# The first segment's layer norm: its root on ScalarE and VectorE, its loads on two queues, its order changed

## The chip, the cores and the metric

The kernel runs on one core of a Trainium2 chip. The metric is the device time of one execution in microseconds (us), lower is better. A core has five engines that work side by side, each with its own stream of instructions, taken in order: TensorE (PE, matrix multiplication; its weight loads are listed apart as PEld), VectorE (DVE), ScalarE (ACT), GpSimd (POOL) and SyncE (SP), which here only starts DMA transfers. ScalarE can start transfers too, from a queue of its own. Engines wait for each other and for transfers by semaphores.

## The reference

```python
x = A_x                                     # 2048 tokens of 640 features, bf16
xn = (x - mean(x)) / sqrt(var(x) + 1e-05)    # layer norm of each token
q, k, v = xn @ wq, xn @ wk, xn @ wv          # 32 heads of 20
# four segments of 512 tokens, in order:
#   p = softmax(q k^T / sqrt(20) + causal mask);  a_dot = p v
#   a_mem = phi(q) M / (phi(q) z + 1e-06)        # M, z: sums over earlier segments
#   o = g * a_mem + (1 - g) * a_dot              # g = sigmoid(beta)
#   M += phi(k)^T v ; z += sum of phi(k)
s = o @ wo
h = sigmoid(xn @ w_gate) * (xn @ w_up)       # 1536 wide
out = x + s * silu(h @ w_down)
```

## The kernel before

Tokens are handled in four segments of 512, each in four blocks of 128. The features (640) are five chunks of 128. A projection therefore is five matmuls that add into one PSUM tile. The PSUM tiles of all stages but the scores come from one ring of four buffers (`ps_d`).

The order of each engine's instructions is the order in which the program writes them (`manual_schedule`). The middle part of the program is written by a planner with due times (`TIMES`); the beginning, which the change touches, is written out by hand:

- Lines 137 to 164: the loads. All go out from SP's queue: x in blocks 0, 1, 2, then the first column half of `Wv`, x block 3, the second half of `Wv`, then `Wk`, `Wq` and `beta`. `load_x` (line 137) takes a list of blocks.
- Lines 166 to 183: GpSimd fills constants, among them `mhalf` (-0.5, the power of the root) and `ident` (for transposes).
- Lines 225 to 239: `ln_stats` (VectorE: two `bn_stats` over 320 columns each, then `bn_aggr`, which gives mean and variance `mv`), `ln_rstd` (GpSimd: add EPS, then power -0.5, giving `rs`), `ln_norm` (VectorE: subtract the mean, multiply by `rs`, giving `xn`).
- Line 246, `ln_transpose`: five transposes on TensorE into a PSUM tile `pT`, then a copy by ScalarE or VectorE into `xnT`. `first_transpose` (line 642) is the same for block 0, in two parts: three chunks copied by ScalarE, two by VectorE.
- Line 330, `do_V(n, j, half, engine)`: the V projection of a block for half of the columns (five matmuls of 320 columns into `psv`), copied by the engine named.
- Line 629, `keep_warm(k)`: k matmuls on a tile of zeros, whose results nobody reads.
- Lines 633 to 693: the order of the first segment. Statistics run one or two blocks ahead of the norm; then transposes and V projections alternate; then the five K projections (`do_K`, copied by VectorE) and the five Q projections (`do_Q`, copied by ScalarE) follow, both into `psq` tiles. Their weights are `Wk` and `Wq`. In between, ScalarE's queue starts the loads of `Wg` and `Wu` (1920 KB each), and GpSimd's `late_constants` (line 186) waits for the last `xn` before it fills the constants of later stages.
- Lines 694 to 709: `bound` (rows that bound the scores, by way of DRAM tile `Bd` into `QT`), gates, and the first five gate and up projections of the GLU (`gp`, `up`), with Tanh on ScalarE (`tg`, line 410) and a product on VectorE (`hT`, line 421).

Behind that the planner's part begins with the first scores (line 535). It mixes scores, attention, GLU and the next segments' projections; those segments' norms use `ln_stats`, `ln_rstd` and `ln_norm` as well, with GpSimd's power.

Of the kernel before, what the change touches and what calls it, by code (L numbers as in the profile page):

```python
# [9 lines left out]
P = 128  # L10
D = 640
# [9 lines left out]
EPS = 1e-5  # L21
SCALE = DH ** (-0.5)
HD = D // 2

BF = mybir.dt.bfloat16
F32 = mybir.dt.float32
ACT = mybir.ActivationFunctionType
# [28 lines left out]
def segment_units(n):  # L56
# [11 lines left out]
    stats0=(0.83, 1.2, 1.95, 3.9), stats=(-0.55, 0.42, 1.32, 3.57), norm=(5.2, 5.75, 6.03, 6.18),  # L68
# [13 lines left out]
def kernel(  # L82
# [14 lines left out]
    nc = tc.nc  # L97
# [3 lines left out]
    cpool = ctx.enter_context(tc.tile_pool(name="const", bufs=1))  # L101
    ps_s = ctx.enter_context(tc.tile_pool(name="ps_s", bufs=1, space=PSUM))
    ps_d = ctx.enter_context(tc.tile_pool(name="ps_d", bufs=4, space=PSUM))
    lnp = ctx.enter_context(tc.tile_pool(name="ln", bufs=2))
# [19 lines left out]
    xt_of, xnT_of = {}, {}  # L124

    def mm(out_, lhsT, rhs, start, stop):


        if not ORDER["columns"]:
            nc.tensor.matmul(out_, lhsT=lhsT, rhs=rhs, start=start, stop=stop, skip_group_check=True)  # L130
            return
        for r in range(4):
            cols = slice(32 * r, 32 * r + 32)
            nc.tensor.matmul(out_[cols], lhsT=lhsT[:, cols], rhs=rhs, start=start, stop=stop,  # L134
                             tile_position=(0, 32 * r), skip_group_check=True)

    def load_x(n, parts=((0, 4),)):
        if n not in xt_of:
            xt_of[n] = lnp.tile([P, 4, D], BF, name="xt4", bufs=3)
        src = x2[n * L:(n + 1) * L, :].rearrange("(j p) d -> p j d", p=P)  # L140
        for a, b in parts:
            nc.sync.dma_start(xt_of[n][:, a:b, :], src[:, a:b, :])

    def load_w(eng, dst, src):
        eng.dma_start(dst[:], src.rearrange("(c p) n -> p c n", p=P))
# [3 lines left out]
    Wv = cpool.tile([P, DC, D], BF, name="Wv")  # L149
# [5 lines left out]
    warm = stg.tile([P, 3 * L], BF, name="mn")  # L155
    nc.vector.memset(warm[:, 0:L], 0.0)
    beta_b = cpool.tile([P, H], BF, name="beta_b")
    for half, blocks in ((0, (0, 1, 2)), (1, (3,))):
        load_x(0, [(j, j + 1) for j in blocks])
        hs = slice(half * HD, (half + 1) * HD)  # L160
        nc.sync.dma_start(Wv[:, :, hs], A_wv[:, hs].rearrange("(c p) n -> p c n", p=P))
    load_w(nc.sync, Wk, A_wk)
    load_w(nc.sync, Wq, A_wq)
    nc.sync.dma_start(beta_b[:], A_beta.partition_broadcast(P))

    mhalf = cpool.tile([P, 4], F32, name="mhalf")
    nc.gpsimd.memset(mhalf[:], -0.5)
    ident = cpool.tile([P, P], BF, name="ident")
# [17 lines left out]
    def late_constants(after):  # L186
        nc.gpsimd.tensor_copy(Mbd[:, 0, 0:1], after[:, 0:1])
        nc.gpsimd.memset(Ind[:], -1.0)
        nc.gpsimd.affine_select(out=Ind[:], in_=Ind[:], compare_op=ALU.is_ge, fill=0.0, base=0,
                                pattern=[[P, DC], [-DH, 4], [-4 * DH, NG]], channel_multiplier=1)  # L190
        nc.gpsimd.affine_select(out=Ind[:], in_=Ind[:], compare_op=ALU.is_ge, fill=0.0, base=DH - 1,
                                pattern=[[-P, DC], [DH, 4], [4 * DH, NG]], channel_multiplier=-1)
        nc.gpsimd.memset(KT[:].bitcast(mybir.dt.uint32), 0x3F803F80)
        ones_columns(1)
        nc.gpsimd.memset(obs[0][:], 0.0)
        nc.gpsimd.memset(Mbd[:], 1.0)
        for c, (h0, h1) in enumerate(HEADS):
            t = Mbd[:, c, :].rearrange("p (h e) -> p h e", e=E1)
            base = P * c - DH * h0
            nc.gpsimd.affine_select(out=t, in_=t, compare_op=ALU.is_ge, fill=0.0, base=base,  # L200
                                    pattern=[[-DH, 8], [0, E1]], channel_multiplier=1)
            nc.gpsimd.affine_select(out=t, in_=t, compare_op=ALU.is_ge, fill=0.0, base=DH - 1 - base,
                                    pattern=[[DH, 8], [0, E1]], channel_multiplier=-1)
        for r, c0, c1, w in WINDOWS:
            rows = slice(32 * r, 32 * r + 32)
            nc.gpsimd.tensor_copy(BD[rows, c0:c1, :], Mbd[rows, c0:c1, w * E1:w * E1 + WIN])
        nc.gpsimd.memset(Mbd[:], 0.0)
# [17 lines left out]
    def ln_stats(n, j, mv):  # L225
        st = lnp.tile([P, 2, 6], F32, name="st")
        for i in range(2):
            nc.vector.bn_stats(st[:, i, :], xt_of[n][:, j, i * HD:(i + 1) * HD])
        nc.vector.bn_aggr(mv[:, j, :], st[:])

    def ln_rstd(mv, rs, sl):
        nc.gpsimd.tensor_scalar(rs[:, sl], mv[:, sl, 1], EPS, None, op0=ALU.add)
        nc.gpsimd.tensor_tensor(rs[:, sl], rs[:, sl], mhalf[:, sl], op=ALU.pow)

    def ln_norm(n, j, mv, rs):
        xn = lnp.tile([P, D], BF, name="xn", bufs=2)
        nc.vector.tensor_scalar(xn[:], xt_of[n][:, j, :], mv[:, j, 0:1], rs[:, j:j + 1],
                                op0=ALU.subtract, op1=ALU.mult)
        return xn

    def ln_tiles(n):
        mv = lnp.tile([P, 4, 2], F32, name="mv")
        rs = lnp.tile([P, 4], F32, name="rs")
        return mv, rs

    def ln_transpose(n, j, xn, eng):
        if n not in xnT_of:
            xnT_of[n] = xpool.tile([P, DC, L], BF, name="xnT")
        pT = ps_d.tile([P, DC, P], BF, name="pT", tag="d")
        for c in range(DC):  # L250
            nc.tensor.transpose(pT[:, c, :], xn[:, c * P:(c + 1) * P], ident[:])
        dst = xnT_of[n][:, :, j * P:(j + 1) * P]
        if eng is nc.scalar:
            nc.scalar.copy(dst, pT[:])  # L254
        else:
            nc.vector.tensor_copy(dst, pT[:])
# [10 lines left out]
    def new_seg(n):  # L267
        seg[n] = dict(kt=stg.tile([P, DC, L], BF, name="ktd"),
                      kabs=stg.tile([P, DC], F32, name="kabs", bufs=2), hT=[], aa={}, odot=None)
# [60 lines left out]
    def do_V(n, j, half, evac):  # L330
        ps = ps_d.tile([P, HD], F32, name="psv", tag="d")
        for k in range(DC):
            mm(ps[:], xnT_of[n][:, k, j * P:(j + 1) * P], Wv[:, k, half * HD:(half + 1) * HD],
               k == 0, k == DC - 1)
        dst = V[n % 2][:, j, half * 16:(half + 1) * 16, 0:DH]
        src = ps[:].rearrange("p (h e) -> p h e", e=DH)
        if evac is nc.scalar:
            nc.scalar.copy(dst, src)
        else:
            nc.vector.tensor_copy(dst, src)  # L340
# [288 lines left out]
    def keep_warm(k):  # L629
        for _ in range(k):  # L630
            nc.tensor.matmul(wps[:], lhsT=warm[:, 0:P], rhs=warm[:, 0:L], start=True, stop=True)

    keep_warm(11)
    mv, rs = ln_tiles(0)
    new_seg(0)
    xns = {}

    def stats0(j):
        ln_stats(0, j, mv)
        ln_rstd(mv, rs, slice(j, j + 1))  # L640

    def first_transpose():

        xnT_of[0] = xpool.tile([P, DC, L], BF, name="xnT")
        for c0, c1 in ((0, 3), (3, 5)):
            pT = ps_d.tile([P, c1 - c0, P], BF, name="pT", tag="d")
            for c in range(c0, c1):
                nc.tensor.transpose(pT[:, c - c0, :], xns[0][:, c * P:(c + 1) * P], ident[:])
            dst = xnT_of[0][:, c0:c1, 0:P]
            if c0:  # L650
                nc.vector.tensor_copy(dst, pT[:])
            else:
                nc.scalar.copy(dst, pT[:])

    def norm0(j):
        xns[j] = ln_norm(0, j, mv, rs)

    stats0(0)
    stats0(1)
    norm0(0)  # L660
    first_transpose()
    load_w(nc.scalar, Wg, B_w_gate)
    stats0(2)
    norm0(1)
    keep_warm(2)
    do_V(0, 0, 0, nc.scalar)
    ln_transpose(0, 1, xns[1], nc.scalar)
    load_w(nc.scalar, Wu, B_w_up)
    stats0(3)
    norm0(2)  # L670
    do_V(0, 0, 1, nc.scalar)
    do_V(0, 1, 0, nc.scalar)
    ln_transpose(0, 2, xns[2], nc.scalar)
    norm0(3)
    late_constants(xns[3])
    do_V(0, 1, 1, nc.scalar)
    do_V(0, 2, 0, nc.scalar)
    ln_transpose(0, 3, xns[3], nc.scalar)
    do_V(0, 2, 1, nc.scalar)
    do_V(0, 3, 0, nc.scalar)  # L680
    do_V(0, 3, 1, nc.scalar)
# [7 lines left out]
    relayout(0, 0, Kd, KT, nc.sync)  # L689
    relayout(0, 0, Qd, QT, nc.sync)  # L690
    load_x(1)
    for c in range(3, 5):
        do_Q(0, c, nc.scalar)
# [46 lines left out]
    for p in range(0, OLD, 5):  # L740
        n, g = units[p][0], units[p][1][0][0]
# [22 lines left out]
    st = {}  # L764
# [12 lines left out]
    for n in range(NSEG):  # L777
# [52 lines left out]
        if n + 2 < NSEG:  # L830
            on("load_x", 0, load_x, (n + 2,))
# [106 lines left out]
```

## Time and profile before

| | |
|---|---|
| median of 3 runs | 322.85 us (322.77 to 323.37) |
| the profiled execution | 323.07 us |
| its span, from first to last instruction | 321.3 us |
| TensorE clock granted, mean | 1.00 |
| HBM read and written | 19.90 MB and 14.78 MB |
| ScalarE's idle time before its first copy of `xnT` | 4.2 us |
| VectorE's wait for the first x block | 2.0 us |
| VectorE's idle time before the first copy of K | 5.3 us |

How to read what the prediction shows: in the table of busy times, each engine has busy time, share of the span and count of instructions. In the chain of waits, each line is the start (us from the start of the span), the duration, and what the end of the kernel hung on in that stretch: an engine with tile and source line, or a transfer. It is followed back from the last instruction. In the timeline each line has start, duration, engine, source line, operation, output <- inputs, shapes and count, and in brackets the idle time of the engine just before and what ended it; the engine ACTq or SPq is the issue of a transfer. In the list of groups, the figures behind the bar are busy time in us and mean ns of one, then idle time before them. "issue" is time in which the engine waited for nothing that the profile shows.

### The profile page before, as it was taken

The page shows a single profiled execution, that of the slowest core. Times are in us where ns is not written, and L with a number is a line of the kernel's source. Part 1 is how long each engine was busy: PE and PEld are TensorE (multiplying, and loading weights), DVE is VectorE, ACT ScalarE, POOL GpSimd, SP SyncE. Part 2 cuts the span into 40 slices and gives each one's busy share as a digit, 9 for nine tenths or more (in the row PEclk, how much of TensorE's full clock was granted, in tenths as well). Part 3 has the DMA queues.
Part 4 walks back from the last instruction along what each step waited for, and adds up shares of the span by engine and source line. Part 5 has one row for each costly group of instructions (what it writes and reads, how often), then busy time and mean ns, then how long its engine had stood idle before and what let it go on. Part 6 is the DMA issues. An engine that isn't in the chain of part 4 may idle for free.

```text
span 321.3 us, 10065 instructions
## 1 busy us (share of the span) xinstructions
PE 313.3 (98%) x4247; PEld 167.2 (52%) x4247; DVE 229.8 (72%) x501; ACT 223.6 (70%) x221; POOL 137.6 (43%) x232
## 2 busy tenths in 40 slices
PE   7999999999999999999998999999999999999995
PEld 2544434665545445654565455545466655445673
DVE  5284265765779888997778999977787686744465
ACT  2623468788798777777897868779797775777630
POOL 4870035525273445335453364444633353535322
PEclk9999999999999999999999999999999999999999
DMA  7987479330742462506593482435554000270312
GB/s 216 380 333 182 133 158 339 119 57 2 210 153 61 91 173 84 124 22 194 160 212 96 114 121 94 114 109 174 138 140 128 23 22 22 103 146 4 98 19 82
DMA packets 55797, 41.36 MB, mean 129 GB/s; under 512 B 26920, under 2 KB 54376, under 8 KB 55752
## 3 DMA queue, kind: packets, MB, share of 16 engines
q1 hardware_dynamic: 54440, 36.78, 43.1%
q10 hardware_dynamic: 1312, 3.93, 3.1%
q8 instruction: 33, 0.54, 0.7%
q14 instruction: 12, 0.10, 0.1%
HBM read 19.90 MB, written 14.78 MB: 108 GB/s over the span
## 4 chain that ended last, share of the span: by engine, by line
PE 92%; DVE 2%; ACT 2%; POOL 1%; issue 1%; DMA 1%; DVEq 0%; ACTq 0%
PE yp L130 11%; PE up L130 11%; PE gp L130 10%; PE psq L130 9%; PE Sps L535 8%; PE gp L134 6%; PE up L134 5%; PE yp L134 5%; PE ApsT L559 5%; PE psv L130 4%; PE psq L134 4%; PE sp L130 3%; PE sp L134 3%; PE psv L134 1%; PE sp L516 1%; ACT pt L543 1%
## 5 line engine op out<-in xcount | busy, mean ns | idle before, releaser
L543 ACT ACTIVATE pt<-Sps 128x2048 bf16<-128x2048 f32 (+1 forms) x81 | 150.3, 1856 | 42.5 <-PE Sps L535 38.9
L545 POOL TENSOR_SCALAR_AFFINE_SELECT pt<-pt 128x512 bf16<-128x512 bf16 x128 | 82.7, 661 | 160.1 <-ACT pt L543 160.0
L421 DVE SCALAR_TENSOR_TENSOR hT<-tg,up 128x512 bf16<-128x512 bf16 x48 | 32.3, 673 | 23.1 <-PE up L130 8.5
L130 PE MATMUL up<-xnT,Wu 128*128 128x512 bf16 x160 | 43.0, 380 | 0.1
L130 PE MATMUL yp<-Wd,hT 128*128 128x320 bf16 x257 | 40.3, 300 | 1.2 <-issue 1.2
L410 ACT ACTIVATE tg<-gp 128x512 bf16<-128x512 f32 x48 | 28.6, 596 | 16.7 <-PE gp L130 12.7
L130 PE MATMUL gp<-xnT,Wg 128*128 128x512 bf16 x150 | 39.3, 380 | 0.0
L535 PE MATMUL Sps<-QT,KT 23*128 23x128 bf16 (+3 forms) x512 | 32.7, 301 | 0.1
L578 DVE STREAM_TRANSPOSE obT<-ob 128x512 bf16<-128x512 bf16 x30 | 21.1, 704 | 12.8 <-POOL ob L574 12.8
L130 PEld LDWEIGHTS <-hT 128*128 128x128 bf16 x257 | 23.5, 98 | 13.1 <-issue 4.5
L438 DVE SCALAR_TENSOR_TENSOR aa<-t,yp 128x320 bf16<-128x320 bf16 x32 | 15.4, 481 | 13.9 <-ACT t L437 13.7
L134 PE MATMUL gp<-xnT,Wg 128*32 128x512 bf16 x360 | 24.1, 380 | 0.0
L580 DVE STREAM_TRANSPOSE tb<-ApsT 128x512 f32<-128x512 f32 x30 | 21.2, 708 | 3.2 <-PE ApsT L559 3.0
L130 PEld LDWEIGHTS <-Wu 128*128 128x128 bf16 x160 | 14.4, 97 | 16.3 <-issue 3.2
L559 PE MATMUL ApsT<-pt,V 128*32 128x512 bf16 (+2 forms) x480 | 22.8, 299 | 0.0
L130 PEld LDWEIGHTS <-Wg 128*128 128x128 bf16 x150 | 14.0, 98 | 16.3 <-issue 2.2
L535 PEld LDWEIGHTS <-KT 23*128 23x128 bf16 x512 | 9.7, 92 | 24.4 <-issue 24.1
L134 PE MATMUL up<-xnT,Wu 128*32 128x512 bf16 x320 | 21.7, 380 | 0.0
L437 ACT ACTIVATE t<-yp 128x320 bf16<-128x320 f32 x32 | 13.9, 435 | 10.8 <-PE yp L130 9.0
L130 PE MATMUL psv<-Wv,xnT 128*128 128x320 bf16 x130 | 20.9, 299 | 0.4 <-ACT xnT L254 0.3
L574 POOL TENSOR_TENSOR ob<-tb,rb 128x320 bf16<-128x320 f32 x27 | 19.7, 731 | 2.2
L134 PE MATMUL yp<-Wd,hT 128*32 128x320 bf16 x508 | 20.2, 300 | 0.0
(114 smaller groups left out, 448.4 us busy)
## 6 DMA issues: line engine op xcount, KB each, us to landing
KT<-Kd SPq DMA_DIRECT2D x32, 80.0 KB
QT<-Qd SPq DMA_DIRECT2D x32, 80.0 KB
out_dram<-xt SPq DMA_DIRECT2D x15, 160.0 KB
Wg<-in_B_w_gate_dram ACTq DMA_DIRECT2D x1, 1920.0 KB
Wu<-in_B_w_up_dram ACTq DMA_DIRECT2D x1, 1920.0 KB
xt<-in_A_x_dram SPq DMA_DIRECT2D x3, 640.0 KB
Wd<-in_B_w_down_dram SPq DMA_DIRECT2D x1, 1920.0 KB
Xd<-xn SPq DMA_DIRECT2D x12, 160.0 KB
```

What stands on the lines that cost most here:

```text
L130: nc.tensor.matmul(out_, lhsT=lhsT, rhs=rhs, start=start, stop=stop, skip_group_check=True)
L134: nc.tensor.matmul(out_[cols], lhsT=lhsT[:, cols], rhs=rhs, start=start, stop=stop, tile_position=(0, 32 * r), skip_group_check=True)
L410: nc.scalar.activation(tg[:], gp[:], ACT.Tanh, scale=0.5)
L421: nc.vector.scalar_tensor_tensor(out=h[:], in0=seg[n]["tg"][:], scalar=1.0, in1=up[:], op0=ALU.add, op1=ALU.mult)
L438: nc.vector.scalar_tensor_tensor(out=s["aa"][j][:, hs], in0=t2[:], scalar=1.0, in1=yp[:], op0=ALU.add, op1=ALU.mult)
L535: nc.tensor.matmul(Sps[:, r, c0:c0 + ncol], lhsT=KT[32 * r:32 * r + DH + 3, g, kb * P:(kb + 1) * P], rhs=QT[32 * r:32 * r + DH + 3, g, q0: ...
L543: nc.scalar.activation(pt[:, :, 0:ntot], Sps[:, :, 0:ntot], ACT.Exp, scale=SCALE)
L545: nc.gpsimd.affine_select(out=pt[:, :, c0:c0 + P], in_=pt[:, :, c0:c0 + P], compare_op=ALU.is_ge, fill=0.0, base=0, pattern=[[0, 4], [1, P ...
L559: nc.tensor.matmul(ps[32 * r:32 * r + 32, q0:L], lhsT=Vflat[n % 2][:, off:off + 32], rhs=t[:, r, c0:c0 + ncol], start=(i == 0), stop=(i == ...
L574: nc.gpsimd.tensor_tensor(ob[:, :, 0:DH], tb[:, :, 0:DH], rb[:].unsqueeze(2).to_broadcast([P, L // 32, DH]), op=ALU.mult)
L578: nc.vector.transpose(s["obT", g // 4][:, g % 4, :], ob[:].rearrange("p b e -> p (b e)"))
L580: s["turn", g] = (lambda: nc.vector.transpose(tb[:].rearrange("p b e -> p (b e)"), ps[:]), quotients, turn_back)
```

## The change

Only the first segment is touched. Its loads are divided among SP's and ScalarE's queues, and block 0 is loaded in two column halves, one from each queue. Its root is no longer GpSimd's add and power: ScalarE takes a square root with EPS as bias (`root0`, from a tile `epsc` that GpSimd fills), and VectorE takes the reciprocal at the head of `norm0`. Statistics are written out by halves and stand elsewhere in VectorE's order. The transposes of block 3 move ahead of `do_V(0, 2, 0)`, and their copy goes to VectorE. Nine instead of eleven warm matmuls stand at the beginning. The later segments keep GpSimd's root.

```diff
-    def load_x(n, parts=((0, 4),)):
+    def load_x(n, a=0, b=4, cols=slice(0, D), eng=nc.sync):
...
-        for a, b in parts:
-            nc.sync.dma_start(xt_of[n][:, a:b, :], src[:, a:b, :])
+        eng.dma_start(xt_of[n][:, a:b, cols], src[:, a:b, cols])
...
-    for half, blocks in ((0, (0, 1, 2)), (1, (3,))):
-        load_x(0, [(j, j + 1) for j in blocks])
+
+    def load_wv(half, eng):
         hs = slice(half * HD, (half + 1) * HD)
-        nc.sync.dma_start(Wv[:, :, hs], A_wv[:, hs].rearrange("(c p) n -> p c n", p=P))
+        eng.dma_start(Wv[:, :, hs], A_wv[:, hs].rearrange("(c p) n -> p c n", p=P))
+
+    load_x(0, 0, 1, slice(0, HD))
+    load_x(0, 0, 1, slice(HD, D), nc.scalar)
+    load_x(0, 1, 2)
+    load_wv(0, nc.scalar)
+    load_x(0, 2, 3)
+    load_x(0, 3, 4, eng=nc.scalar)
+    load_wv(1, nc.sync)
...
+    epsc = cpool.tile([P, 1], F32, name="epsc")
+    nc.gpsimd.memset(epsc[:], EPS)
...
-    keep_warm(11)
+    keep_warm(9)
     mv, rs = ln_tiles(0)
     new_seg(0)
-    xns = {}
-
-    def stats0(j):
-        ln_stats(0, j, mv)
-        ln_rstd(mv, rs, slice(j, j + 1))
+    xns, sts = {}, {}
+
+    def half_stats0(j, i):
+        if i == 0:
+            sts[j] = lnp.tile([P, 2, 6], F32, name="st")
+        nc.vector.bn_stats(sts[j][:, i, :], xt_of[0][:, j, i * HD:(i + 1) * HD])
+        if i == 1:
+            nc.vector.bn_aggr(mv[:, j, :], sts[j][:])
+
+    def root0(j):
+        nc.scalar.activation(rs[:, j:j + 1], mv[:, j, 1:2], ACT.Sqrt, bias=epsc[:])
...
     def norm0(j):
+        nc.vector.reciprocal(rs[:, j:j + 1], rs[:, j:j + 1])
         xns[j] = ln_norm(0, j, mv, rs)
 
-    stats0(0)
-    stats0(1)
+    half_stats0(0, 0)
+    half_stats0(0, 1)
+    root0(0)
+    half_stats0(1, 0)
     norm0(0)
+    half_stats0(1, 1)
     first_transpose()
+    root0(1)
+    norm0(1)
     load_w(nc.scalar, Wg, B_w_gate)
-    stats0(2)
-    norm0(1)
+    half_stats0(2, 0)
+    half_stats0(2, 1)
     keep_warm(2)
     do_V(0, 0, 0, nc.scalar)
     ln_transpose(0, 1, xns[1], nc.scalar)
+    root0(2)
     load_w(nc.scalar, Wu, B_w_up)
-    stats0(3)
     norm0(2)
+    half_stats0(3, 0)
+    half_stats0(3, 1)
     do_V(0, 0, 1, nc.scalar)
     do_V(0, 1, 0, nc.scalar)
     ln_transpose(0, 2, xns[2], nc.scalar)
+    root0(3)
     norm0(3)
     late_constants(xns[3])
     do_V(0, 1, 1, nc.scalar)
+    ln_transpose(0, 3, xns[3], nc.vector)
     do_V(0, 2, 0, nc.scalar)
-    ln_transpose(0, 3, xns[3], nc.scalar)
     do_V(0, 2, 1, nc.scalar)
     do_V(0, 3, 0, nc.scalar)
     do_V(0, 3, 1, nc.scalar)
```

## The prediction

> **What bounds the kernel now.** I read the page's busy times first, then the chain of waits in order of time, then the timeline of the first 30 us, then the groups for single prices.
>
> ```profile
> span 321.3 us, 10065 instructions
> PE 313.3 (98%) x4247; PEld 167.2 (52%) x4247; DVE 229.8 (72%) x501; ACT 223.6 (70%) x221; POOL 137.6 (43%) x232
> ```
>
> TensorE is busy for all but 8.0 us of the span. Whatever delays its dense stream delays the end; other engines matter only where TensorE waits for them. The chain of waits says where that is:
>
> ```profile
> 0.80 2.40 DMA xt<-in_A_x_dram
> ...
> 3.21 0.90 DVE st L228 x2
> ...
> 4.13 0.22 DVE mv L229
> ...
> 4.44 0.26 POOL rs L232
> ...
> 4.77 0.59 POOL rs L233
> ...
> 5.39 0.46 DVE xn L237
> ...
> 13.25 1.53 PE psv L130 x10
> 14.78 10.79 PE psq L130 x50
> ```
>
> Up to about 10 us the chain hops from the first load over VectorE and GpSimd to the first transposes and back; from 14.78 us it is TensorE almost alone until 316 us. Among TensorE's waits the profile blames only one behind 14.78 us on another engine (cps, 0.3 us); the other, 1.2 us, is issue. So the measure of this change is one moment: when the K projections (psq) begin, 14.62 us by the timeline. All behind it should shift rigidly. The timeline's anchors are:
>
> ```profile
> 0.79 1.28 ACT L653 ACT_TABLE_LOAD   x1 [0.79 <-PEq L922]
> 5.89 0.45 PE L648 MATMUL pT<-ident,xn 128*128 128x128 bf16 x5 [0.40 <-DVE xn L237]
> 8.08 0.45 PE L251 MATMUL pT<-ident,xn 128*128 128x128 bf16 x5 [0.34 <-DVE xn L237]
> 8.57 0.69 ACT L254 COPY xnT<-pT 128x640 bf16<-128x640 bf16 x1 [0.37 <-PE pT L251]
> 10.01 0.44 PE L251 MATMUL pT<-ident,xn 128*128 128x128 bf16 x5
> 11.97 0.44 PE L251 MATMUL pT<-ident,xn 128*128 128x128 bf16 x5
> 14.62 5.56 PE L130 MATMUL psq<-xnT,Wk 128*128 128x512 bf16 x25
> 26.69 0.60 ACT L410 ACTIVATE tg<-gp 128x512 bf16<-128x512 f32 x1 [0.49 <-PE gp L130]
> ```
>
> Call the four groups of transposes T0 to T3: 5.89, 8.08, 10.01, 11.97. The table load at 0.79 waits for nothing: ScalarE is idle until 6.27.
>
> **The change, part by part.**
>
> *Root.* The path loses GpSimd's add and power: from mv0 at 4.34 to the norm at 5.39 is 1.05 us. It gains a Sqrt on ScalarE and a reciprocal on VectorE. No Sqrt stands in the trace. Nearest is a 128x32 Tanh; the reciprocal has rows at 16 and 8 elements:
>
> ```profile
> L216 ACT ACTIVATE th<-beta_b 128x32 f32<-128x32 bf16 x1 | 0.2, 221 | 0.0
> L567 DVE RECIPROCAL rb<-tb 128x16 f32<-128x16 f32 x30 | 7.4, 248 | 0.4
> L618 DVE RECIPROCAL rd<-Aps 128x8 f32<-128x8 f32 x2 | 0.4, 200 | 0.0
> ```
>
> Sqrt: 0.22, the ScalarE row with the fewest columns; bounds 0.15 (VectorE's copy of 8 columns, 147 ns) and 0.37 (ScalarE's copy of 256 columns). Reciprocal: 48 ns less for 8 elements fewer gives 0.16 for one; bounds 0.10 and 0.20. A crossing between engines is 0.03 to 0.10 here (mv to GpSimd 0.10, GpSimd to norm 0.04, xn to PE 0.05); I take 0.08 into ScalarE and 0.05 out. Without anything else block 0 would gain 1.05 - (0.08 + 0.22 + 0.05 + 0.16 + 0.02) = 0.52 us.
>
> *Table load.* Sqrt makes a second function set necessary. In the built program ScalarE's order is three DMA issues, the wait for mv0, the table load, Sqrt: the Sqrt has two waits (mv0 and GpSimd's epsc), the first stands alone ahead of the load. So the load no longer hides in the idle start; its 1.28 us fall behind mv0. Block 0: mv0 4.34, ScalarE awake 4.42, load to 5.70, Sqrt 5.72 to 5.94, reciprocal 5.99 to 6.15, norm 6.17 to 6.62 (0.45), T0 6.67 instead of 5.89: +0.78.
>
> The Trainium skill (ScalarE: Activation LUTs, What ACT_TABLE_LOAD costs) says a switch costs a load of about 1.28 us and a drain of 1.38 us, 2.66 us together, and its next section advises against mixing exp and sqrt. The trace has the same 1.28 and shows no drain, as nothing ran before; by the page's sum the forecast below would be 1.4 us higher.
>
> *Second load.* The first Tanh needs the old set again; its load stands behind the last Q copy. There ScalarE idles 0.49 us before tg at 26.69, so tg comes 0.8 us late and hT (27.85, waiting for up) some 0.3 us late; with th in between, cb 0.4 late. TensorE doesn't wait for these: its next buffers are due a microsecond later. Bd<-cb waits in the queue behind the 640 KB x load in any case (issued 29.16, its readers at 34.35). Cost 0; without that cover 0.4, since the first scores start right behind the bound rows.
>
> *Blocks 1 to 3.* VectorE now stops at each reciprocal until ScalarE has done the root, and ScalarE does it only behind the copy of the block before. Behind the waiting reciprocal stand the norm, the next statistics and the copy of xnT. Block 1: second statistics 6.62 to 7.07, mv1 7.30; ScalarE copies xnT 7.05 to 7.53 (T0 + 0.38, 0.48 long), root 7.55 to 7.77, reciprocal to 7.98, norm 8.00 to 8.39 (0.39), T1 8.44 (+0.36: some of the delay goes into the 0.34 us for which PE waited there). Block 2: copy of xnT1 8.93 to 9.62 (T1 + 0.49, 0.69), root 9.64 to 9.86, reciprocal to 10.07, norm to 10.49 (0.40), T2 10.54 (+0.53); before, this norm was done at 9.37, long ahead. Block 3: copy of xnT2 11.06 to 11.76, root to 12.00, reciprocal to 12.21, norm to 12.66 (0.39 to 0.45), T3 12.72.
>
> *T3 ahead of V(2,0).* Before, V(1,1) and V(2,0) stood between T2 and T3. Now only V(1,1) does, done at 10.54 + 0.39 + 0.69 = 11.62; so TensorE idles about 1.1 us for T3. Behind it come four half V's of 0.69 (14.62 - 13.25 = 1.37 for two) after T3's 0.39: psq at 12.72 + 0.39 + 2.74 = 15.85, against 14.62: **+1.23 us**. Block 3's copy moves to VectorE (some 0.7 us), hidden behind V(2,0) and V(2,1); ScalarE is spared one copy where it had time.
>
> *Loads.* SP loses three issues of about 0.45, ScalarE gains three, done by 2.2, when it is idle. First bytes move at 1.8 to 2.0 and x0's 164 KB are in by 2.5; its statistics began at 3.21. Two halves at once share the same DMA engines: gain between -0.2 (smaller packets) and +0.3 us; I take 0. Now Wv0 (410 KB) runs beside x1 and x2. At the 224 GB/s of the slowest stretch at nearly full DMA share (3.0 to 3.2 us), x1 with an equal share of Wv0 is in by 1.85 + 492/224 + 0.65 = 4.7, wanted at 6.0; both halves of Wv with all of x (1474 KB) by 9.1, wanted at 8.83: 0 to 0.3 lost; 0 taken, as the mean rate of the first 7 us was higher. Wg and Wu are issued 1.4 to 2 us later, behind roots, but last bytes were in by about 22.5 and gp begins at 25.4. GpSimd's late constants start 2 us later and have until 24.7 (KT's memset, done at 13.8 before) or much longer.
>
> *Two warm matmuls fewer.* The last warm ones end near 5.0; T0 at 6.67 leaves TensorE idle 1.7 us, against 0.40 before. The page grants full clock in every slice, yet the weight loads of the warm matmuls come 0.43 us apart, and 11 took only 4.25 us, so the last ran at half that: full speed came near 4.85, 3.5 us after the start. Nine just reach it. I take 0; a clock lost again costs up to half of another 3.5 us, 1.75.
>
> The Trainium skill (TensorE: Matmul & The Clock Gate, What's actually happening) puts the fall back after an idle window of about 3.4 us, which 1.7 us wouldn't fill; but it says that the window runs free, so a shorter burst may miss it.
>
> **Sum.** The profiled execution took 323.07: span 321.3 and 1.77 around it. Span 321.3 + 1.23 = 322.53, with 1.77 is 324.30. That execution lay 0.22 above the median of the runs, 322.85, so I forecast 322.85 + 1.23 = **324.1 us**. Each root and each reciprocal counts four times, since T0 to T3 hang on each other: Sqrt of 0.15 gives -0.3, of 0.37 +0.6; reciprocals -0.24 to +0.16; landing -0.3 to +0.2; Wv up to +0.3. They will not all fall to one side: about +0.6 to +2.1, 323.4 to 324.9.
>
> **Rivals.** (1) *The load is off the path* (not slower). If the table is in by 4.4, because ScalarE's load somehow runs ahead of the wait, the same sum gives T0 5.4, T1 7.2, T2 9.3; the T3 chain is 0.5 to 0.7 longer than before, and psq starts at 14.6: 322.9, or 322.5 if the halves also land 0.3 sooner. For it: ScalarE idles from 2.2 on. Against: the order in the program. It decides from a load that ends by 4.42. (2) *TensorE turns cold* in the 1.7 us gap or doesn't get warm: V groups of 1.3 instead of 0.69 in the first 3 us, part of it hidden in the waits for T1 to T3; about +1.0: 325.1, at most 325.9. For it: nine matmuls end just after the change of pace. Against: the gaps of 0.40 and 0.34 us before did no harm, and only one is longer now. That the change doesn't do what it says is excluded by the program's order.
>
> **Numbers.** Forecast 0.70, rival (1) 0.16, rival (2) 0.14. A measurement of this kernel can tell 0.2% (0.65 us) from no change. The forecast's low end is within it (0.05 of 0.70); rival (1) is mostly no change (0.12), some faster (0.04). Slower 0.65 + 0.14 = 0.79, same 0.17, faster 0.04. The range, 323.2 to 325.2, leaves out most of (1) and the worst of (2).
>
> **What would show it.** ACT_TABLE_LOAD starting at about 4.4, a second one before the first tg; T0 to T3 near 6.7, 8.4, 10.5, 12.7; TensorE idle for about 1.1 us ahead of T3, released by xn; psq at 15.9; its spacing behind unchanged. It is wrong if the load starts near 2, if psq starts before 15.2, or if the span grows by something else than psq's delay.

## The result, and the profile after

The changed kernel takes 324.06 us (median of 12 executions, 323.01 to 325.72); the kernel before, run beside it, 323.11 (12 executions, 322.77 to 324.22). The ratio is 1.0032, 95% interval 1.0016 to 1.0048: slower by 0.5 to 1.6 us. The profiled execution of the changed kernel is the slowest of its twelve, 325.72, with a span of 324.0 us; that has to be kept in mind in what follows.

The busy times of the changed kernel's page:

```profile
span 324.0 us, 10039 instructions
PE 312.1 (96%) x4216; PEld 168.0 (52%) x4245; DVE 230.9 (71%) x506; ACT 225.1 (69%) x225; POOL 134.6 (42%) x225
```

TensorE does the same work less two warm matmuls, and idles 11.9 us instead of 8.0 by the trace. Part of the difference probably only seems so: 29 more matmul records are missing here, 13 of them of `up`, and the trace has six idle stretches of 0.16 us ahead of `up` that the trace of before doesn't have. The chain of waits of the changed kernel (start, duration, what) shows where the front spends its time:

```profile
3.14 0.90 DVE st L651 x2
...
4.07 0.22 DVE mv L653
...
4.36 1.28 ACT L656
5.65 0.30 ACT rs L656
...
5.98 0.17 DVE rs L672
...
6.18 0.46 DVE xn L247
...
6.68 0.71 PE pT L664 x5
```

The line `ACT L656` of 1.28 us, right behind `mv` and ahead of the root `rs`, is the table load. GpSimd is gone from the chain (it had 0.26 and 0.59 there), and a load of 1.28, a root of 0.30 and a reciprocal of 0.17 have come instead. The timeline of the changed kernel gives the anchors, first ScalarE's load and Sqrt, then TensorE:

```profile
4.36 1.28 ACT L656 ACT_TABLE_LOAD   x1 [4.36 <-DVE mv L653]
5.65 0.29 ACT L656 ACTIVATE rs<-mv,epsc 128x1 f32<-128x1 f32 x1
...
1.24 4.02 PE L641 MATMUL wps<-mn 128*128 128x512 bf16 x9 [1.24 <-DVE mn L155]
6.68 0.71 PE L664 MATMUL pT<-ident,xn 128*128 128x128 bf16 x5 [1.42 <-DVE xn L247]
7.19 1.06 PE L641 MATMUL wps<-mn 128*128 128x512 bf16 x2
8.04 1.54 PE L130 MATMUL psv<-Wv,xnT 128*128 128x320 bf16 x5
...
11.77 0.45 PE L261 MATMUL pT<-ident,xn 128*128 128x128 bf16 x5
12.06 0.84 PE L130 MATMUL psv<-Wv,xnT 128*128 128x320 bf16 x5
13.96 0.45 PE L261 MATMUL pT<-ident,xn 128*128 128x128 bf16 x5 [1.06 <-DVE xn L247]
...
16.97 5.56 PE L130 MATMUL psq<-xnT,Wk 128*128 128x512 bf16 x24
```

T0 stands at 6.68, as worked out. But its five transposes take 0.71 us where before they took 0.45, two warm matmuls 1.06 instead of 0.59, five matmuls of V 1.54 instead of 0.84: TensorE runs at half pace here, until about 10 us. So this execution shows both the wait for the table and the second rival, and its K projections begin at 16.97 instead of 14.62. The wait ahead of T3 (13.96) is there too, 1.06 us, released by `xn`.

### The profile page after: what moved, and what is told of

It reads as the page before. It is cut to its first block, busy times and chain, and to the rows that moved or that the text cites. A ratio compares the mean times of both kernels' runs of the same rounds, so it can differ in the third digit from the quotient of the medians.

```text
span 324.0 us, 10039 instructions
## 1 busy us (share of the span) xinstructions
PE 312.1 (96%) x4216; PEld 168.0 (52%) x4245; DVE 230.9 (71%) x506; ACT 225.1 (69%) x225; POOL 134.6 (42%) x225
## 4 chain that ended last, share of the span: by engine, by line
PE 78%; DMA 7%; ACT 5%; DVE 5%; issue 2%; SPq 2%; POOL 1%; ACTq 0%; DVEq 0%
PE yp L130 9%; PE psq L130 9%; PE Sps L545 7%; PE up L130 7%; PE gp L130 6%; PE gp L134 5%; PE ApsT L569 5%; PE up L134 5%; PE yp L134 5%; PE psv L130 4%; PE psq L134 4%; DMA Wd<-in_B_w_down_dram 3%; PE sp L130 3%; PE sp L134 3%; ACT pt L553 2%
## 5 line engine op out<-in xcount | busy, mean ns | idle before, releaser
L130 PE MATMUL up<-xnT,Wu 128*128 128x512 bf16 x147 | 40.3, 379 | 1.3 <-issue 0.9
L130 PE MATMUL gp<-xnT,Wg 128*128 128x512 bf16 x144 | 38.1, 379 | 0.3 <-issue 0.2
```

## The experiments

Each was timed against the kernel before on one chip with it (12 executions of each experiment if nothing else is said); ratios are to the kernel before. The theory, called the path theory: the start of the K projections (psq) decides, and it hangs on the table load behind `mv0`, on the norms' new order, and on T3's place. Its rivals: TensorE's pace alone, and the loads. Three more came up on the way.

**1. The table load taken off the path.**

```diff
     keep_warm(9)
+    pre = cpool.tile([P, 1], F32, name="pre")
+    nc.scalar.activation(pre[:], epsc[:], ACT.Sqrt)
```

> The changed kernel with one Sqrt of the constant epsc added on ScalarE right behind its three DMA issues, so that the table load does not stand behind mv0. Path theory (the load's 1.28 us lie on the path to the first norm, and everything to the K projections hangs on it): first Sqrt of a variance ends near 4.7, T0 at about 5.4 (changed kernel 6.68), K projections at about 14.7 to 15.0 where the changed kernel's clock is full, total 322.8 to 323.4, ratio to before 0.999 to 1.001. Rival, the clock (the load is harmless, the lost TensorE clock makes all of the loss): the gap ahead of T0 closes here too, so the same total, but then e2 must give it as well. Rival, the loads (two queues delay something later): no gain over the changed kernel, 324.0.

Measured: 322.60 us, ratio 0.9992 (0.9974 to 1.0009). ScalarE's timeline in this kernel:

```profile
2.29 1.28 ACT L645 ACT_TABLE_LOAD   x1 [2.29 <-issue]
3.58 0.20 ACT L645 ACTIVATE pre<-epsc 128x1 f32<-128x1 f32 x1
4.27 0.29 ACT L658 ACTIVATE rs<-mv,epsc 128x1 f32<-128x1 f32 x1 [0.48 <-DVE mv L655]
```

The load now lies in idle time, the first variance's root begins 1.4 us earlier than in the changed kernel, T0 stands at 5.29 and psq at 14.38. One instruction more takes the whole loss away. It doesn't by itself part the table from the pace, because the gap ahead of T0 closes as well; for that there is the next.

**2. More warm matmuls in the gap.** `keep_warm(9)` becomes `keep_warm(14)`.

> The changed kernel with 14 warm matmuls in front of T0 instead of 9, so that TensorE does not idle for 1.4 to 1.7 us there. Path theory: T0 stays at 6.7 and T3 still waits, K projections at 15.9 in every execution; executions above 325 vanish, the median stays near 324.2 (ratio 1.003). Clock rival: the loss vanishes, total 322.9 to 323.3. Loads rival: 324.0, as the changed kernel.

Measured: 323.99, ratio 1.0044 (1.0026 to 1.0061). TensorE runs at full pace from T0 on, and T0 (6.81), the wait ahead of T3 (1.06) and psq (15.90) stay late. The pace alone is out as the cause. Executions above 325 did not vanish, though: the profiled one, 325.64, has psq only 1.28 us later than before and ends 2.6 later. This is TensorE's list of waits in it up to 60 us (total, times, longest):

```profile
PE pT L261 <- DVE xn L247: 1.1, 1, 1.1
PE yp L134 <- DMA Wd<-in_B_w_down_dram: 1.0, 1, 1.0
```

The first down projection waits 1.0 us for `Wd`, as it does for 0.5 us in the changed kernel's profile.

**3. T3 behind V(2,0) again.**

```diff
-    ln_transpose(0, 3, xns[3], nc.vector)
     do_V(0, 2, 0, nc.scalar)
+    ln_transpose(0, 3, xns[3], nc.vector)
```

> The changed kernel with the transposes of block 3 put back behind V(2,0); their copy stays on VectorE. Path theory: the wait of 1.06 us ahead of T3 is filled with V(2,0), psq 0.6 to 0.7 us earlier than in the changed kernel at the same clock, median 323.3 to 323.6. Clock and loads rivals: the wait ahead of T3 cost nothing that counts at the end, 324.0.

Measured: 323.94, ratio 1.0027 (1.0007 to 1.0047): close to the rivals' 324.0, but the interval holds both expectations, so the time doesn't decide. The trace says more: the wait is gone and psq is earlier, as the path theory has it. TensorE's timeline:

```profile
11.76 0.45 PE L261 MATMUL pT<-ident,xn 128*128 128x128 bf16 x5
12.05 1.80 PE L130 MATMUL psv<-Wv,xnT 128*128 128x320 bf16 x10
13.95 0.45 PE L261 MATMUL pT<-ident,xn 128*128 128x128 bf16 x5
```

T2 and T3 stand where they stood in the changed kernel (11.77 and 13.96, also after a start at half pace), but ten matmuls instead of five lie between them and no wait. psq begins at 16.36, 0.61 us earlier.

**4. The loads alone**, put into the kernel before: its `load_x`, `load_wv` and the seven load lines of the change.

> The kernel before with only the loads of the change (two queues, block 0 in column halves). Path theory: statistics begin 0 to 0.3 us earlier, K projections 0 to 0.3 us earlier, total 322.7 to 323.1 (ratio 0.999 to 1.000). Loads rival: 323.5 or more, with a later wait of TensorE for a transfer (Wd or QT) that before does not have.

Measured: 322.73, ratio 0.9991 (0.9972 to 1.0010); T0 5.83, psq 14.55, no wait for a transfer. The loads do no harm; a gain of 0.06 us at T0 is as small as the spread among traces.

**5. The changed kernel once more.**

> The changed kernel once more, unchanged, for a second trace. Path theory: T0 at 6.6 to 6.7 and a wait of 1.06 us ahead of T3 whatever the clock does; K projections at 15.9 if TensorE turns to full speed before 5 us, near 17.0 if not. Clock rival: with full speed early, psq below 15.2. Ratio to before 1.002 to 1.005.

Measured: 323.81, ratio 1.0040 (1.0023 to 1.0057), T0 6.64, T3 13.77 after a wait of 1.11, psq 16.78. Here the pace was lost in a second way. The granted clock by the microsecond, the third figure from the right in each line (behind it DMA share and GB/s):

```profile
7.00:8.00 1.00, 0.97 (x7) 0.38 (x5) 0.65 (x4) 0.67 (x2) 0.00 (x0) 0.92 1.06 396
8.00:9.00 1.00, 1.00 (x8) 0.62 (x6) 1.00 (x3) 0.13 (x1) 0.00 (x0) 0.50 1.07 390
9.00:10.00 1.00, 1.00 (x8) 0.64 (x6) 0.37 (x2) 0.90 (x3) 0.00 (x0) 0.50 1.07 366
10.00:11.00 1.00, 1.00 (x5) 0.55 (x4) 0.65 (x3) 0.55 (x3) 0.00 (x0) 0.50 1.13 361
11.00:12.00 1.00, 1.00 (x11) 0.76 (x10) 0.96 (x3) 0.42 (x2) 0.00 (x0) 0.88 1.01 306
```

T0 still ran at full pace (0.45 us); a gap of 1.73 us lay ahead of it, and from 7.8 to 11.2 us the clock is at one half.

**6. Both repairs in one** (the edits of 1 and 3).

> The table load ahead of the wait (as e1) and T3 behind V(2,0) (as e3), both in one. Path theory: the two costs add, T0 at 5.3, T2 at 9.2, T3 at 11.4 with a wait of 0.2 to 0.3 us ahead of it, psq at 13.8 (14.38 in e1, 14.62 in before), ratio to before 0.997 to 0.999. A rival that later waits for transfers take back what the start gains: psq at 13.8, but the first down projection (yp) waits for Wd and the ratio is 0.999 to 1.001.

Measured: 322.43, ratio 0.9983 (0.9969 to 0.9996): faster than before. psq 14.06, not 13.8, as T0 and the warm pair behind it still ran at half pace. No wait for `Wd`.

**7. The second table load hidden as well.**

```diff
     do_V(0, 3, 1, nc.scalar)
+    back = cpool.tile([P, 1], F32, name="back")
+    nc.scalar.activation(back[:], epsc[:], ACT.Tanh)
```

> As e6, with one Tanh of epsc behind the last V copy, so that the second table load falls into ScalarE's idle 6 us of the K projections. Path theory: tg 0.8 us earlier relative to psq, and nothing else: ratio as e6 within 0.001. A rival, the second load (it delays hT, cb and the chain of transfers to Wd): 0.2 to 0.6 us less than e6, and no wait for Wd.

Measured: 322.00, ratio 0.9973 (0.9960 to 0.9986): the fastest of all, and faster than both kernels. TensorE's timeline around T2 and T3:

```profile
9.35 0.45 PE L261 MATMUL pT<-ident,xn 128*128 128x128 bf16 x5
...
11.54 0.45 PE L261 MATMUL pT<-ident,xn 128*128 128x128 bf16 x5
...
13.95 3.83 PE L130 MATMUL psq<-xnT,Wk 128*128 128x512 bf16 x16
```

Without the load on the path T2 and T3 stand 2.4 us earlier than in the changed kernel's profile, and psq at 13.95, 0.67 ahead of before. Whether the hidden Tanh has a part in it can't be told: the intervals of 6 and 7 overlap.

**8 and 9. The second load hidden in the changed kernel, alone**, by the same two lines, measured twice.

> The changed kernel with the same Tanh behind the last V copy: the second table load alone is hidden. Path theory: no more than 0.2 us less than the changed kernel, ratio 1.002 to 1.005. Second-load rival: waits for Wd vanish, ratio 1.001 or less.

Measured: 325.21 (6 executions), ratio 1.0073 (1.0051 to 1.0095), worse than the changed kernel, which neither theory had. In its trace the load is hidden and tg comes 0.8 us earlier relative to psq; psq is at 16.72 after a start at half pace. Three of the six executions had a mean granted clock of 0.992 to 0.993, the sign of the loss seen in 5, but they are the three shortest of the six (324.06, 324.43, 325.10), so that loss doesn't explain the high median.

> The changed kernel with the second table load hidden, a second time, since its first measurement (1.0073) lies above the changed kernel's (1.0040). Path theory: the hidden load can only help, by 0 to 0.3 us; the first measurement met more executions with a slow TensorE start; ratio 1.002 to 1.005. Rival, the load among the K projections harms by itself: ratio above 1.006 again.

Measured: 324.05, ratio 1.0037 (1.0013 to 1.0061), the changed kernel's own value; psq 16.97. The first measurement was not repeated; why it was high is not known. The second load costs nothing that these runs can tell. ScalarE in the changed kernel, for comparison:

```profile
28.56 1.28 ACT L420 ACT_TABLE_LOAD   x1
...
29.86 0.60 ACT L420 ACTIVATE tg<-gp 128x512 bf16<-128x512 f32 x1
```

tg starts 12.89 us after psq, against 12.07 before: the 0.8 us late that were worked out, with nobody on TensorE waiting.

**10. T3's early place alone**, put into the kernel before (`ln_transpose(0, 3, xns[3], nc.vector)` ahead of `do_V(0, 2, 0)`).

> The kernel before with only the transposes of block 3 ahead of V(2,0), copied by VectorE. Path theory: there the last norm is ready at 10.6, ahead of T3, so its early place costs nothing by itself; T3 at 11.0 without a wait, psq at 14.3 to 14.6 (two waits of 0.15 for ScalarE's copies shrink to one), ratio 0.998 to 1.000. Rival, T3's place costs by itself: psq 0.5 us later or more, ratio 1.002.

Measured: 322.51, ratio 0.9991 (0.9973 to 1.0010). TensorE's timeline:

```profile
11.00 0.44 PE L251 MATMUL pT<-ident,xn 128*128 128x128 bf16 x5
11.32 2.89 PE L130 MATMUL psv<-Wv,xnT 128*128 128x320 bf16 x20
14.05 3.62 PE L130 MATMUL psq<-xnT,Wk 128*128 128x512 bf16 x15
```

T3 doesn't wait; the same line that costs the changed kernel a wait of 1.06 us here brings psq 0.57 us forward (14.05; I had expected at least 14.3). So the order costs only together with a late norm.

**11. The changed kernel with the loads of before.**

> The changed kernel with the loads of before (one queue, whole blocks). Path theory: statistics begin 0 to 0.1 us later, everything else as in the changed kernel: T0 at 6.7, ratio 1.003 to 1.005. Loads rival: the loss of the changed kernel comes from its loads, ratio 1.002 or less.

Measured: 323.91, ratio 1.0036 (1.0014 to 1.0058). The statistics begin at 3.09, so the two halves brought nothing. This is the trace in which the changed order ran at full pace from T0 on:

```profile
6.63 0.45 PE L662 MATMUL pT<-ident,xn 128*128 128x128 bf16 x5 [1.36 <-DVE xn L245]
6.92 0.59 PE L639 MATMUL wps<-mn 128*128 128x512 bf16 x2
7.54 0.85 PE L130 MATMUL psv<-Wv,xnT 128*128 128x320 bf16 x5
8.41 0.45 PE L259 MATMUL pT<-ident,xn 128*128 128x128 bf16 x5
9.05 1.53 PE L130 MATMUL psv<-Wv,xnT 128*128 128x320 bf16 x10 [0.18 <-DMA Wv<-in_A_wv_dram]
10.53 0.45 PE L259 MATMUL pT<-ident,xn 128*128 128x128 bf16 x5
10.81 0.84 PE L130 MATMUL psv<-Wv,xnT 128*128 128x320 bf16 x5
12.71 0.45 PE L259 MATMUL pT<-ident,xn 128*128 128x128 bf16 x5 [1.06 <-DVE xn L245]
13.01 2.88 PE L130 MATMUL psv<-Wv,xnT 128*128 128x320 bf16 x20
15.72 2.11 PE L130 MATMUL psq<-xnT,Wk 128*128 128x512 bf16 x8
```

T0 to T3 at 6.63, 8.41, 10.53, 12.71: the forecast's 6.67, 8.44, 10.54, 12.72.

**12. Eleven warm matmuls again** in the changed kernel.

> The changed kernel with 11 warm matmuls again. Path theory: T0 stays at 6.65; two matmuls more leave a gap of about 0.7 to 1.2 us where there were 1.4 to 1.7, so executions with a slow start get fewer: ratio 1.002 to 1.004, psq 15.9 or up to 1.1 later. Clock rival: ratio 1.001 or less.

Measured: 323.25, ratio 1.0021 (1.0004 to 1.0037). T0 6.64, T3 12.82, psq 15.83, full pace from within T0 on (its transposes took 0.55 us); ten of its 12 executions lie between 322.98 and 323.51. The changed kernel in 5, which ran on another chip, spreads over 322.99 to 325.58. Two warm matmuls left out are thus a likely part of the loss, but not shown alone: the intervals overlap, and 14 of them (run 2) did not do better.

The marks of all traces in us. "Pace" says whether T0 and the first V ran at full pace; the last column but one is TensorE's wait in the stretch from 168 to 174 us.

| kernel | T0 | T3 | wait ahead of T3 | psq | pace | wait for Wd | wait near 170 | span |
|---|---|---|---|---|---|---|---|---|
| before | 5.89 | 11.97 | none | 14.62 | full | none | 1.15 | 321.3 |
| changed | 6.68 | 13.96 | 1.06 | 16.97 | half | 0.49 | 0.29 | 324.0 |
| 1 table early | 5.29 | 11.38 | 1.06 | 14.38 | full | none | 0.54 | 320.9 |
| 2 warm 14 | 6.81 | 12.89 | 1.06 | 15.90 | full | 1.00 | 0.81 | 323.9 |
| 3 T3 later | 6.67 | 13.95 | none | 16.36 | half | none | 0.22 | 322.3 |
| 4 loads alone | 5.83 | 11.90 | none | 14.55 | full | none | 0.42 | 320.6 |
| 5 changed again | 6.64 | 13.77 | 1.11 | 16.78 | lost | none | 0.96 | 323.4 |
| 6 early, T3 | 5.28 | 11.65 | none | 14.06 | half at T0 | none | 0.69 | 320.2 |
| 7 and Tanh | 5.29 | 11.54 | none | 13.95 | half at T0 | none | 0.30 | 319.7 |
| 8 Tanh | 6.64 | 13.72 | 1.06 | 16.72 | half | none | 1.20 | 323.9 |
| 9 Tanh again | 6.68 | 13.97 | 1.06 | 16.97 | half | none | 0.27 | 322.8 |
| 10 T3 alone | 5.91 | 11.00 | none | 14.05 | full | none | 0.56 | 320.0 |
| 11 old loads | 6.63 | 12.71 | 1.06 | 15.72 | full | none | none | 321.4 |
| 12 warm 11 | 6.64 | 12.82 | 1.06 | 15.83 | full | none | none | 321.4 |

## Why the prediction was right, and where it was not

**The table load behind mv0** was right in place and size: forecast 4.42 to 5.70, measured 4.36 to 5.64. Run 1 shows that without it the loss is gone, and run 2 that the loss stays where TensorE keeps its pace. The Trainium skill (ScalarE: Activation LUTs, What ACT_TABLE_LOAD costs) had set a drain of 1.38 us beside the load of 1.28; the trace agrees with the load and shows no such drain, as the Sqrt starts 0.01 us after the load's end and the second load 0.01 us after the copy ahead of it. The forecast's sum by the row was the better one.

**Sqrt and reciprocal.** The Sqrt took 0.29 to 0.30, not 0.22; the reciprocal 0.16, as the line through 16 and 8 elements said. The 0.07 at block 0 went unseen because the statistics began 0.07 earlier; in the later blocks the root starts 0.1 us ahead of the end of ScalarE's copy, which makes up for it. Two small errors met.

**T0 to T3** held within 0.04 us in the trace at full pace (run 11), and psq's shift there is 1.10, 1.21 in run 12, 1.28 in run 2, where 1.23 was forecast. The wait for T3 was forecast as about 1.1 and is 1.06. VectorE's copy of block 3 took 0.49, not 0.7; it was hidden either way.

**Loads and second load** were set at nothing, and runs 4, 9 and 11 found nothing. One term was seen the wrong way round: I feared that `Wv` would come late on two queues; it came late on one (0.18 us in run 11, 0.32 in run 10).

**Two warm matmuls fewer** is the step that failed. I took 0 and gave the rival 0.14. Of the six traces with nine warm matmuls and T0 at 6.6 to 6.7 (changed, 3, 5, 8, 9, 11), five ran at half pace for some 3 us, and psq shifted by up to 2.35. "Nine just reach it" rested on one execution; in the fourteen traces the first full pace begins anywhere from 4.3 us (run 4) to 10.6 (run 3). The last section shows what it goes by: with only nine warm matmuls and the gap that the table load leaves behind them, four of the six came to it late, at 9.5 to 10.6 us, and run 5 lost it again.

**"All behind it should shift rigidly"** did not hold to a few tenths. From psq to the end of the span it is 306.7 us in before, and between 305.6 (run 12) and 308.0 (run 2) in the others. Two waits make most of the difference: that for `Wd`, which the trace of before doesn't have, and one near 170 us, from none to 1.20. Both differ between executions of kernels whose instructions there are the same. The forecast took the 1.2 us of "issue" in the profile of before, which is the wait near 170, for a fixed part of the span.

The traces suggest what that wait is. TensorE's wait there in the kernel before, and then in run 8:

```profile
170.60 0.31 PE L130 MATMUL yp<-Wd,hT 128*128 128x320 bf16 x1 [1.15 <-issue]
```

```profile
173.12 1.52 PE L130 MATMUL psv<-Wv,xnT 128*128 128x320 bf16 x10 [1.20 <-DVE tb L590]
```

In the kernel before, it falls between two matmuls of yp, and the profile finds nothing that the second waits for. The packets of DMA queue q8, which the profile lists as `instruction` (33 in the kernel before, of 16 KB each), fit it: in all twelve traces with the wait TensorE goes on 1.37 to 1.54 us after the end of such a packet, whether the wait was 0.22 us long or 1.20. The place of the wait also moves with the number of warm matmuls: ahead of the first of five matmuls of yp with 14 of them (run 2), ahead of the fifth in the kernel before with 11, behind all five with nine. So TensorE most likely waits there for its own next instructions, and not for `tb`, which the profile names in some traces. No run tests this, and why the packet comes sooner or later stays open; so does whether a later start shortens the wait: with psq at 16.72 it was 1.20 (run 8), with psq at 16.97 it was 0.27 (run 9).

**The total** was in part luck. The twelve executions of the changed kernel lie in two groups, five from 323.01 to 323.37 and five from 324.21 to 324.65, with one at 323.91 and one at 325.72; the forecast of 324.1 stands between the groups, and so does the median. Kept and lost pace would make two such groups, the lower one held down by a shorter wait near 170 than in the profile of before: run 11's trace, at full pace and without that wait, took 323.16, though psq was 1.10 late. But only one execution of each run has a trace, so this account of the groups is not shown.

## What to carry to other kernels

A function from another table set brings its load (1.28 us here) to wherever its first call stands. If that call has two waits, one of them can stand ahead of the load, as `mv` does here; a call on a constant, made while ScalarE is idle, moves the load away (run 1). When a helper engine's latency is cut out of a chain, look at what now waits in order: here each norm came to stand behind a copy of the block before, and a reordering that does no harm by itself (run 10) became a wait. A burst of warm matmuls should last until the first real work, not only until the moment at which the pace changed in one trace.

## What the runs showed of the hardware

The granted clock does not show the half pace at the start. The changed kernel between 8 and 9 us, in the same columns as in run 5:

```profile
8.00:9.00 1.00, 1.00 (x5) 0.60 (x4) 0.96 (x4) 0.00 (x0) 0.00 (x0) 1.00 1.07 390
```

It says 1.00 while five matmuls of 320 columns take 1.54 us instead of 0.84. The trace's own list of clock changes, which no view prints as it is, begins only with the first full pace (at 9.98 us in this trace, at 4.74 in the kernel before), and the view counts what lies ahead of that as 1.00. Up to there only the pace of equal matmuls tells; a loss later on (run 5) is shown.

Its entries also show what the pace goes by. All but the last, which the end of the trace cuts, last a whole number of steps of 3.41 us (run 5: full from 4.42, half from 7.83, full from 11.24), and the place of the steps against the start of the program differs from trace to trace. Counting the steps back from the entries, and TensorE's idle time in each by the modelled ends of its matmuls, gives the same picture in all fourteen traces: the first full pace begins at the end of the first step in which TensorE idled no more than 0.58 us (run 8, 6.06 to 9.47); the step before it there, with 0.79 us idle, didn't bring it, nor did any with more. Full pace was kept through a step with 1.41 us idle (run 11, 5.17 to 8.58) and lost after one with 1.76 (run 5, 4.42 to 7.83). Where between these values the limits lie, no run shows. Nine warm matmuls at half pace last 4.02 us, little more than one step, and the idle 1.4 us behind them spoil the next: in the changed kernel's profile the step from 3.16 to 6.57 has 1.31 us idle, and full pace came one step later.

The Trainium skill (TensorE: Matmul & The Clock Gate, What's actually happening) lets the clock fall back after an idle window of about 3.4 us. The trace agrees with the length, 3.41 us, but in run 5 the clock fell after a step in which TensorE idled 1.76 us and had been busy again for 1.2 us: that the window has to be idle throughout does not fit.
